# Linear-memory attention and a leaky two-layer network in one Trainium2 kernel: another layout for phi, keys and values, and another order at three places

## The chip, the cores and the metric

The kernel runs on one core of one Trainium2 chip. A core has five engines with an instruction queue each: PE (TensorE, the matrix unit; its weight loads are listed apart as PEld), DVE (VectorE), ACT (ScalarE), POOL (GpSimd) and SP (SyncE, which here only issues loads and stores). PE writes to PSUM, which has eight banks; everything else lies in SBUF. The metric is the time of one execution on the device in microseconds (us). The measurement of the kernel before has a median of 709.62 us over three runs (708.53 to 710.71).

## The reference

All inputs are float32, but the two weight matrices, which are float64. B = 8 batches, H = 8 heads, S = 576 tokens, D = 64, M = 32 memory slots, 512 -> 2048 -> 512 for the network.

```python
a = exp(phi - max(phi, axis=2)); a = a / sum(a, axis=2)      # softmax over the 32 slots, per token
k_m = einsum('bhsm,bhsd->bhmd', a, k)                       # keys folded into 32 slots
v_m = einsum('bhsm,bhsd->bhmd', a, v)                       # values folded into 32 slots
scores = q @ k_m.T / sqrt(64)                               # 576 x 32 per head
attn = softmax(scores)                                      # over the 32 slots
x = (attn @ v_m), heads side by side                        # 4608 tokens x 512
h = x @ w_in;  g = maximum(0.01 * h, h);  out = g @ w_out
```

In the kernel the softmax over phi is taken over tokens (axis 2 of phi is the token axis): a maximum and a sum over the 576 tokens for each of the 256 pairs of head and slot. Values are never multiplied out: `v_m` is folded into `w_in` for each batch, so that the first layer works on `attn` straight away.

## The kernel before

**Steps.** Work is written as small steps with names, and the order in which the program issues them is the order on every engine. The steps of batch b are `a{b}.`:

- `phi`, `kv0`, `kv1`, `q0`, `q1`: the loads, all issued on SP, with 96 partitions of six tokens each (CP = 96, NJ = 6). They go into the pool "ld" of eight buffers, which the pieces of the weights use as well.
- `A1` (DVE): maxima of phi over a partition's six tokens, in five instructions. `A2` (PE): two transposes. `A3` (DVE): the maxima over partitions, put on a diagonal. `B0` (PE): one product that spreads them over all partitions. `B1x` (DVE): subtract. `B2x` (ACT): exponential. `B3` (POOL): sums over the six tokens, in five instructions.
- `C10`, `C11` (PE, L444): the products of exponentials with keys and values, 6 tokens x 4 heads for each of the two head groups g, at four column positions of the array, with 96 rows and 128 columns (keys and values of a head side by side). An fp32 product goes to PE as two pieces, so 48 products stand in the profile as 96. `C2` (PE): two transposes of the sums. `C3` (DVE): reciprocals, the scaled keys `x_k` and the scaled values `x_v`. `C4` (DVE): a bound on the values.
- `D1` (PE): transposes of `x_k` and `x_v`. `D2` to `D6`: scales and copies (`D3` on ACT copies the keys, `D5` the values). `Q0`, `Q1` (DVE): transposes of the queries, written over buffers of the keys and values.
- `E1` (PE, L567): the scores, at 12 positions of the array, three PSUM banks. `E20` to `E22` (DVE): transposes to SBUF. `S{c}{n}`: the second softmax in chunks of 192 columns ("tb"), on DVE for the first chunks of batch 0 and with POOL otherwise.

The weights come in three pieces a matrix: `i0.ld0` is a load of piece 0 of the first quarter of `w_in`, `o0` is for `w_out`; `y` (ACT), `h` (DVE or ACT) and `t` (DVE) turn float64 into float32, `b` (ACT) squares, `k` (ACT) and `l` (DVE) split a weight into two fp16 parts. `f0j.1` and `f0j.2` fold the values of batch 0 into quarter j and keep the result in fp32; `w0.2`, `w1.1`, `w1.2` and the later `fold` do it for the fp16 parts, with `split` on ACT and DVE.

**Groups and units.** The tokens are worked off in 12 groups of 384 (G = 0 to 11), each in eight units u of 256 hidden columns. A unit is: up products (L750, two PSUM buffers "ph"), leaky activation (ACT, then two instructions on DVE for the fp16 parts), down products (L808, three PSUM banks "po"). Group 0 is done in fp32 while the weights still come in, in an order written out by hand (`OPENING`), in which `u0.P0` is the first half of unit 0's up products, `V` the activation and `O` the down products; `z.n` stands for n idle products. From group 1 on everything is fp16 in three products a tile, in slots: `slot(n)` issues the up products of unit n + 3, the fold that is due (`folds`), its activation, and then the down products of unit n. The steps of the next batches are hung into the slots by three tables (`BEFORE`, `AFTER`, `ENDS`), and so are the fp16 splits of the weights (`SPLIT`). A slot in the steady part takes 5.8 us of PE.

**Buffers in PSUM.** The pool "pa" has three banks. `C10` takes two of them (transposed sums, products), `E1` all three, a fold two.

**The end of a group.** `store` copies a bank "po" to SBUF on ACT (two buffers "ob") and issues four stores of 32 rows for it on SP.

Of the kernel before, what the change touches and what calls it, by code (L numbers as in the profile page):

```python
# [22 lines left out]
A_SCALE = 2.0**13  # L23
# [14 lines left out]
z.14 a0.phi a0.kv1 a0.kv0 a0.A1 a0.A2 a0.A3 a0.q0 a0.B0 z.4 a0.B10 a0.q1 a0.B11 a0.B20 a0.B21  # L38
a0.B3 i0.ld0 a0.C10 a0.C11 a0.Q0 a0.C2 z.4 i0.ld1 i0.ld2 a0.C3 o0.ld0 a0.Q1 a0.D1 i0.y0 i0.h0
a0.D3 i0.t0 a0.D5 a0.E1 i0.y1 i0.h1 i0.t1 i0.y2 o0.ld1 o0.ld2 o1.ld0 a0.E20 i0.h2 a0.E21 a0.S01  # L40
o1.ld1 a0.S11 o0.y0 a0.S02 a0.S12 a0.S03 i0.t2 a0.S13 o1.ld2 o0.y1 a0.S04 f00.1 z.6 a0.S14
i1.ld0 f00.2 a0.S05 o0.h0 a0.S15 i1.ld1 a0.S06 o0.h1 a0.S16 u0.Pa0 o0.y2 a0.E22 u0.Pa1 o0.h2
a0.C4 u0.Pb0 o1.y0 o0.t0 u0.Pb1 u0.V0 a0.D2 o0.t1 u0.V1 i1.ld2 u1.Pa0 o1.y1 a0.D4 i2.ld0 u1.Pa1
# [12 lines left out]
o0.k0 u6.O1 o0.k1 o0.k2 w1.2 u7.O1 o0.l0 o0.l1 o0.l2
# [27 lines left out]
IDLE = (4, 6, 14)  # L84


BEFORE = {2: "A3", 3: "B10", 5: "C3 C4", 7: "D4 D3 D5 D6", 8: "E20 E21 E22", 9: "S03", 11: "S07"}
AFTER = {
    0: "A1", 3: "B20 B3", 6: "Q0 Q1", 8: "S01 S02", 9: "S04 S05", 10: "S06", 11: "S08",
}  # L90
ENDS = {1: "A2", 2: "B0", 4: "C10 C11 C2", 6: "D1 D2", 7: "E1"}
# [3 lines left out]
def kernel(  # L95
# [43 lines left out]
    HP = H // NG  # L139
    ND = D // 32  # L140
# [31 lines left out]
    wo = [const.tile([P, WC], F32, name=f"wo{j}") for j in range(NQ + 1)]  # L172
    wi_s, wo_s = (
# [47 lines left out]
    def weights(kind, j, steps, act):  # L221
# [116 lines left out]
    def attention(b, steps, chunks, f32_chunks=0):  # L338
# [632 lines left out]
```

## Time and profile before

| | |
|---|---|
| median of the runs | 709.62 us (708.53 to 710.71) |
| the profiled execution, whole | 707.58 us |
| its span, first to last instruction | 705.8 us |
| mean granted clock of PE | 0.983 |
| PE busy | 680.9 us, 96% |
| DVE, ACT, POOL busy | 391.6, 266.7, 86.3 us |
| read from HBM, written | 49.81 MB, 9.44 MB |

The page of the profile has the busy share of every engine in 40 slices of the span (17.6 us each), as tenths. A timeline line has the start and the length of a run of like instructions, what was read and written, how many there were, and in brackets how long the engine stood idle before and what released it. A window's line has a stretch of time, its length, then for PE, PEld, DVE, ACT and POOL the busy time and the number of instructions, then the granted clock, the share of the 16 DMA engines and GB/s. In the lines of a single line of code stand the least, median and greatest duration in ns and the start of the first and the last. A piece on PE lasts longer than the distance to the next, since pieces run in a pipeline and side by side.

### The profile page before, as it was taken

What the parts mean: (1) busy time and instruction counts of PE and PEld (TensorE: products, weight loads), DVE (VectorE), ACT (ScalarE), POOL (GpSimd) and SP (SyncE); (2) the same over time, 40 slices, a digit from 0 to 9 for tenths busy, and PEclk for the clock granted to TensorE, in tenths of its full rate; (3) what the DMA queues carried; (4) which work ended last, traced back from release to release, by engine and by line L of the source; (5) the groups of instructions that cost most, each with busy time, mean ns of one, the idle gap of its engine ahead of it and who ended that gap; (6) DMA issues with size and microseconds to landing.
All of it is one profiled execution on the core that took longest, in us unless ns stands there. A gap on an engine that the chain in (4) does not pass through costs nothing.

```text
span 705.8 us, 13103 instructions
## 1 busy us (share of the span) xinstructions
PE 680.9 (96%) x5606; PEld 380.0 (54%) x5606; DVE 391.6 (55%) x618; ACT 266.7 (38%) x426; POOL 86.3 (12%) x82
## 2 busy tenths in 40 slices
PE   6799996999999999999999999999999999999995
PEld 5465544665545545565555545665545545665442
DVE  2884586785797573434684664344594664332220
ACT  1499575562562332421331342321242332321211
POOL 2010230020151120020140020010031030000000
PEclk8699999999999999999999999999999999999999
DMA  9999604904513410303513320304410100100101
GB/s 212 362 385 240 227 0 97 217 1 119 140 25 102 123 25 1 79 1 102 143 37 102 99 48 1 79 1 102 106 41 2 42 5 1 46 1 1 46 1 45
DMA packets 38714, 60.10 MB, mean 85 GB/s; under 512 B 4352, under 2 KB 28928, under 8 KB 38656
## 3 DMA queue, kind: packets, MB, share of 16 engines
q1 hardware_dynamic: 38656, 59.26, 31.5%
q8 instruction: 44, 0.72, 0.4%
q14 instruction: 14, 0.11, 0.1%
HBM read 49.81 MB, written 9.44 MB: 84 GB/s over the span
## 4 chain that ended last, share of the span: by engine, by line
PE 86%; DMA 5%; DVE 4%; ACT 3%; SPq 1%; issue 1%; POOL 0%; ACTq 0%; DVEq 0%; POOLq 0%
PE po L808 50%; PE ph L750 25%; PE pa L662 3%; PE pa L444 3%; PE pa L567 2%; DMA ld<-in_v_dram 1%; DMA ld<-in_moe_w_in_dram 1%; DMA out_dram<-ob 1%; ACT ob L779 1%; SPq L786 1%; DMA ld<-in_phi_dram 1%; ACT W L690 1%; DVE W L691 1%; DVE ld L546 0%; PE pa L404 0%
## 5 line engine op out<-in xcount | busy, mean ns | idle before, releaser
L808 PE MATMUL po<-wo,g 128*128 128x512 f16 (+1 forms) x1680 | 400.6, 392 | 0.3
L808 PEld LDWEIGHTS <-g 128*128 128x128 f16 x1584 | 152.5, 98 | 184.3 <-issue 12.7
L750 PE MATMUL ph<-a,W 128*128 128x192 f16 (+3 forms) x1520 | 210.8, 292 | 5.0 <-ACT gf L757 5.0
L757 ACT ACTIVATE gf<-ph,g_sc 128x384 f32<-128x384 f32 x176 | 98.9, 579 | 229.6 <-PE ph L750 164.2
L765 DVE CAST g<-gf 128x768 f16<-128x768 f32 x88 | 59.9, 681 | 192.7 <-ACT gf L757 192.6
L750 PEld LDWEIGHTS <-W 128*128 128x128 f16 x1440 | 130.3, 98 | 59.6 <-issue 4.4
L766 DVE TENSOR_TENSOR g<-gf,g 128x768 f16<-128x768 f32 x88 | 87.4, 993 | 3.1
L600 POOL TENSOR_TENSOR t<-t,tm 128x1152 f32<-128x1152 f32 (+2 forms) x9 | 16.5, 1833 | 232.5 <-DVE tm L597 232.5
L779 ACT ACTIVATE ob<-po,osc 128x512 f32<-128x512 f32 x29 | 19.7, 688 | 58.7 <-DMA out_dram<-ob 31.6
L662 PE MATMUL pa<-wi,vT 64*32 64x512 f16 (+1 forms) x704 | 32.3, 430 | 2.4 <-DVE t L577 1.9
L691 DVE SCALAR_TENSOR_TENSOR W<-pa,W 128x512 f16<-128x512 f32 x48 | 30.8, 683 | 0.0
L546 DVE STREAM_TRANSPOSE ld<-ld 96x1536 f32<-96x1536 f32 x16 | 27.5, 1752 | 5.8 <-DMA ld<-in_q_dram 5.8
L808 PEld LDWEIGHTS po<-wo,g 128*128 128x128 f32 x96 | 17.5, 190 | 20.8 <-issue 18.7
L434 POOL TENSOR_TENSOR r1k<-r1k,ld 96x256 f32<-96x256 f32 x32 | 27.6, 861 | 2.5
L444 PE MATMUL pa<-ld 96*32 96x128 f32 x768 | 24.9, 286 | 2.8 <-DMA ld<-in_v_dram 2.8
L432 POOL TENSOR_TENSOR r1k<-ld 96x256 f32<-96x256 f32 x8 | 6.5, 815 | 171.0 <-ACT ld L422 171.0
L690 ACT ACTIVATE W<-pa 128x512 f16<-128x512 f32 x48 | 26.1, 599 | 2.7 <-PE pa L662 2.6
L257 ACT ACTIVATE ld<-ld 128x768 f32<-128x768 f32 (+1 forms) x24 | 19.9, 844 | 18.9 <-DMA ld<-in_moe_w_in_dram 16.9
L444 PEld LDWEIGHTS pa<-ld 96*32 96x32 f32 x768 | 22.2, 115 | 7.4 <-issue 3.3
L633 POOL TENSOR_TENSOR a<-t,a 128x1152 f16<-128x1152 f32 (+2 forms) x9 | 18.0, 1999 | 41.4 <-ACT a L629 41.4
L605 ACT ACTIVATE t<-t 128x1152 f32<-128x1152 f32 (+2 forms) x11 | 9.9, 904 | 30.7 <-POOL t L600 30.6
L577 DVE STREAM_TRANSPOSE t<-pa 128x384 f32<-128x384 f32 x24 | 12.3, 556 | 14.3 <-PE pa L567 14.3
(138 smaller groups left out, 421.3 us busy)
## 6 DMA issues: line engine op xcount, KB each, us to landing
ld<-in_k_dram SPq DMA_DIRECT2D x32, 288.0 KB, 5.4
ld<-in_v_dram SPq DMA_DIRECT2D x32, 288.0 KB, 5.7
ld<-in_q_dram SPq DMA_DIRECT2D x16, 576.0 KB, 6.7
out_dram<-ob SPq DMA_DIRECT2D x144, 64.0 KB, 1.7
ld<-in_moe_w_in_dram SPq DMA_DIRECT2D x12, 512.0 KB, 6.2
ld<-in_moe_w_out_dram SPq DMA_DIRECT2D x12, 512.0 KB, 7.2
ld<-in_phi_dram SPq DMA_DIRECT2D x8, 576.0 KB, 7.0
ld<-in_moe_w_in_dram SPq DMA_DIRECT2D x8, 256.0 KB, 7.4
```

The costliest lines, as they stand in the source:

```text
L434: nc.gpsimd.tensor_tensor(s0, s0, ph[:, :, :, j, :], ALU.add)
L444: nc.tensor.matmul(pk[hh * M:(hh + 1) * M, g, :, :], ld["phi"][:, 2 * hh + g, j, :], ld["kv", g, hh // 2][:, :, hh % 2, j, :], start=(j == ...
L546: nc.vector.transpose(flat, ld["q", g].rearrange("p hh j d -> p (hh j d)"))
L662: nc.tensor.matmul(pf[g][cols, :], lhs, rhs, start=(n == 0), stop=(n == len(passes) - 1), tile_position=(g * D, hh * M),)
L690: nc.scalar.activation(w[:, g, 0], src[g], AF.Copy, scale=ws)
L691: nc.vector.scalar_tensor_tensor(w[:, g, 1], src[g], ws, w[:, g, 0], ALU.mult, ALU.subtract)
L750: nc.tensor.matmul(ph[:, t0:t0 + n * SB], lhs, rhs, start=(m == 0), stop=(m == len(seq) - 1))
L757: nc.scalar.activation(dst, ph, AF.Prelu, scale=sc, alpha=SLOPE)
L765: nc.vector.tensor_copy(g[:, 0], gf)
L766: nc.vector.tensor_tensor(g[:, 1], gf, g[:, 0], ALU.subtract)
L779: nc.scalar.activation(ob, po, AF.Copy, scale=so)
L808: nc.tensor.matmul(po, lhs, rhs, start=(f == 0 and m == 0), stop=(f == NQ * NF - 1 and m == len(seq) - 1),)
```

## The change

Phi, keys and values are laid out anew: a head's 576 tokens now fill 64 partitions with nine tokens each (KJ = 9), and the two heads of a pair (hh, g) fill the lower and upper 64 partitions, so all 128 are used. With it

- `A1` and `B3` become one reduction on DVE each (batch 0: `A10` and `A11` for two halves of phi, which are loaded one after the other);
- `A2` and `C2` become one transpose; `B0` becomes two products at two column positions;
- `C10` has 9 x 4 x 2 = 72 products with 64 rows, at four column positions in each of two row halves, into one PSUM bank for each g. For batch 0 keys and values are done apart, `C10` for keys and `C11` for values;
- `C3` is `C30` (DVE, reciprocals), `C3k` (`x_k`, now on ACT) and `C31` (`x_v`, two instructions); `D1` is `D10` and `D11`.

Phi, keys and values of batch 0 are loaded into weight tiles that are not yet in use, and in the order phi, keys, queries, the first quarter of `w_in`, values. `OPENING` is written anew (the idle products too: `z.14` first, then 2, 4, 4, 2, 5, 2, 4), batch 0's first fp32 chunk has two "tb" in place of two chunks of one, and a unit's up products are no longer cut in two halves of tokens. The scales of the folded weights are made once (`fold_scales`) and not in each `split`. At the begin of group 1 the slots issue up products of unit n + 2, none in slot 8, two units in slots 9 and 11. `store` has three buffers, and the stores of the last group go out on SP, POOL and ACT, a bank each.

```diff
-BEFORE = {2: "A3", 3: "B10", 5: "C3 C4", 7: "D4 D3 D5 D6", 8: "E20 E21 E22", 9: "S03", 11: "S07"}
+BEFORE = {
+    2: "A3", 3: "B10", 4: "B3", 5: "C30 C3k C31 C4", 7: "D4 D3 D5 D6", 8: "E20 E21 E22",
+    9: "S03", 11: "S07",
+}
...
+        phi_rows = phi[b].rearrange("h s m -> (h s) m").rearrange(
+            "(hh gp j) m -> gp hh j m", gp=P, j=KJ
+        )
...
-            for j in range(2, NJ):
-                nc.vector.tensor_tensor(mx, mx, phi_t[:, :, j, :], ALU.max)
+            nc.vector.tensor_reduce(
+                var["mx"][:, h0:h1], ld["phi"][:, h0:h1].rearrange("p hh j m -> p hh m j"),
+                AX.X, ALU.max,
+            )
...
+            for g in range(NG):
+                nc.tensor.matmul(
+                    pb[g * D:(g + 1) * D].rearrange("p hh m -> p (hh m)"), ones[:, :D],
+                    var["diag"][:, g], start=True, stop=True, tile_position=(0, g * D),
+                )
...
+            for j in range(KJ):
                 for hh in range(HP):
-                        pk[hh * M:(hh + 1) * M, g, :, :],
-                        ld["phi"][:, 2 * hh + g, j, :],
-                        ld["kv", g, hh // 2][:, :, hh % 2, j, :],
-                        start=(j == 0), stop=(j == NJ - 1), tile_position=(0, hh * M),
+                    for g in range(NG):
+                        rows = slice(g * D, (g + 1) * D)
+                        nc.tensor.matmul(
+                            var["pk"][g][hh * M:(hh + 1) * M, cs], ld["phi"][rows, hh, j, :],
+                            ld["kv", hh][rows, kinds[0]:kinds[-1] + 1, j, :],
+                            start=(j == 0), stop=(j == KJ - 1), tile_position=(g * D, hh * M),
+                        )
...
-                nc.vector.tensor_scalar(
+                nc.scalar.activation(
                     x_k[:, g],
...
+                    AF.Copy, scale=var["r2"][:, 1, g:g + 1],
...
-        ob = ffn.tile([P, E], F32, name="ob", bufs=2)
+        ob = ffn.tile([P, E], F32, name="ob", bufs=3)
+        last = G == len(units) // NU - 1
+        eng = (nc.sync, nc.gpsimd, nc.scalar)[t] if last else nc.sync
...
     def slot(n):
-        m = n + UA
+        if n < NU:
+            ms = [n + 2]
+        else:
+            ms = {NU: [], NU + 1: [n + 1, n + 2], NU + 2: [n + 2], NU + 3: [n + 2, n + 3]}.get(
+                n, [n + UA]
+            )
```

More of the change, by code (lines that the diff above doesn't have):

```diff
@@ L37 @@
 OPENING = """
[L38 to L43, printed above, removed]
@@ L56 @@
-o0.k0 u6.O1 o0.k1 o0.k2 w1.2 u7.O1 o0.l0 o0.l1 o0.l2
+z.14 a0.phi0 a0.phi1 a0.k a0.q0 a0.A10 a0.A11 a0.q1 a0.A2 z.2 a0.A3 a0.B0 z.4 i0.ld0 a0.B10
+a0.B11 a0.B20 a0.B21 i0.ld1 a0.C10 a0.B3 a0.Q0 a0.C2 z.4 i0.ld2 a0.v a0.C30 a0.Q1 a0.C3k a0.D10
+z.2 i0.y0 i0.h0 a0.D3 i0.t0 o0.ld0 a0.E1 z.5 i0.h1 i0.y1 i0.t1 o0.ld1 i0.y2 a0.E20 i0.h2 a0.E21
+i0.t2 o0.ld2 a0.S01 i0.b o1.ld0 a0.E22 a0.C11 z.2 a0.S02 a0.C31 a0.S03 o1.ld1 a0.S11 a0.D11
+o0.y0 a0.S04 a0.S12 a0.D5 o0.h0 o1.ld2 f00.1 z.4 a0.S05 a0.S13 i1.ld0 f00.2 a0.S06 o0.y1 a0.C4
@@ L422, in exp_phi @@
+        def exp_phi(js):
+            part = ld["phi"][:, :, js, :]
             nc.scalar.activation(part, part, AF.Exp)
-        for i in range(parts):
-            steps[f"{name}B1{i}"] = lambda i=i: sub_max(i)
-            steps[f"{name}B2{i}"] = lambda i=i: exp_phi(i)
+        for i in range(len(half) - 1):
+            js = slice(half[i], half[i + 1])
+            steps[f"{name}B1{i}"] = lambda js=js: sub_max(js)
+            steps[f"{name}B2{i}"] = lambda js=js: exp_phi(js)
         @step("B3")
@@ L478, in _ @@
                 )
+        @step("C31")
+        def _():
             var["x_v"] = x_v = att.tile([P, NG, D], F32, name="x_v", bufs=2)
-            nc.vector.tensor_tensor(
-                x_v, pk[:, :, 1, :], r2.unsqueeze(2).broadcast_to([P, NG, D]), ALU.mult
-            )
+            for g in range(NG):
+                nc.vector.tensor_scalar_mul(
+                    x_v[:, g], var["pk"][g][:, D:2 * D], var["r2"][:, 0, g:g + 1]
+                )
         @step("C4")
@@ L722, with up_products @@
     gs = {}
[L724 to L727 removed]
+    def up_products(G, u, i):
+        ph = ps_h.tile([P, GT], F32, name="ph")
         (b0, tb0), (b1, tb1) = blocks(G)
[L729 to L731 removed]
+        if b0 == b1:
             parts = [(b0, tb0, 2, 0)]
@@ L894 @@
         if b + 1 < B:
-            put(ends, n0 + 5, b + 1, "phi kv0 kv1")
+            put(ends, n0 + 5, b + 1, "phi kv0 kv1 kv2 kv3")
             put(ends, n0 + 8, b + 1, "q0 q1")
@@ L917, in slot @@
     def slot(n):
-        m = n + UA
-        rest = []
-        if m < len(units):
+        if n < NU:
+            ms = [n + 2]
+        else:
+            ms = {NU: [], NU + 1: [n + 1, n + 2], NU + 2: [n + 2], NU + 3: [n + 2, n + 3]}.get(
+                n, [n + UA]
+            )
+        rest = []
+        if not ms or ms[0] >= len(units):
+            run(before.get(n, ()))
+        for m in ms:
+            if not NU <= m < len(units):
+                continue
             phs = [up_products(*units[m], i) for i in range(2)]
-            rest = [(b, j, fold(b, j)) for b, j in folds(m)]
-        run(before.get(n, ()))
-        if m < len(units):
+            rest += [(b, j, fold(b, j)) for b, j in folds(m)]
+            if m == ms[0]:
+                run(before.get(n, ()))
             activate(*units[m], phs)
@@ L937 @@
         run(OPENING.split())
-        run(["a2.phi", "a2.kv0", "a2.kv1", "a2.q0", "a2.q1"])
+        run([f"a2.{key}" for key in "phi kv0 kv1 kv2 kv3 q0 q1".split()])
         for n in range(NU - UA, len(units)):
```

223 lines of the change are left out of this document (115 added, 108 removed).

## The prediction

> **What bounds the kernel now.** I read the page first, then the timeline of TensorE over the opening and over the begin of the second group, then the chain of waits and the windows of 5 us there, then single lines in the steady part, and last the end.
>
> ```profile
> span 705.8 us, 13103 instructions
> ...
> PE 680.9 (96%) x5606; PEld 380.0 (54%) x5606; DVE 391.6 (55%) x618; ACT 266.7 (38%) x426; POOL 86.3 (12%) x82
> ...
> PE   6799996999999999999999999999999999999995
> ...
> PEclk8699999999999999999999999999999999999999
> ```
>
> TensorE is busy for 680.9 of 705.8 us. A change can win only in three ways: less work for PE, an earlier start of the dense part (slices 1 and 2 show 6 and 7, and a clock of 0.6 in the second), or removal of the dip in the seventh slice (6). The other engines have room over the whole span. PE's timeline of the opening:
>
> ```profile
> 0.99 5.97 PE L864 MATMUL pa<-ones 128*128 128x128 f32 x28 [0.99 <-POOL ones L165]
> 8.54 0.36 PE L389 MATMUL pa<-ident,r1k 96*128 96x96 f32 x2 [1.58 <-DVE r1k L382]
> 9.96 1.17 PE L404 MATMUL pa<-r1k,ones 128*96 128x256 f32 x2 [1.06 <-DVE r1k L399]
> ...
> 13.62 0.41 PE L444 MATMUL pa<-ld 96*32 96x128 f32 x4 [0.79 <-DMA ld<-in_v_dram]
> 16.02 4.48 PE L444 MATMUL pa<-ld 96*32 96x128 f32 x92 [1.98 <-DMA ld<-in_v_dram]
> ...
> 22.21 0.66 PE L499 MATMUL pa<-ident,x_k 128*96 128x128 f32 x4 [0.48 <-DVE x_k L473]
> ...
> 24.46 1.96 PE L567 MATMUL pa<-ld,kT 32*32 32x192 f32 x96 [1.43 <-ACT kT L513]
> ...
> 31.22 1.92 PE L662 MATMUL pa<-wi,vT 64*32 64x512 f32 x4 [0.49 <-DVE wi L266]
> 33.81 2.93 PE L864 MATMUL pa<-ones 128*128 128x128 f32 x12 [0.67 <-ACT W L678]
> 36.53 3.07 PE L750 MATMUL ph<-a,W 128*128 128x192 f32 x16
> ```
>
> Until 36.53 us, where the first up products start, PE mostly waits: for phi and its maxima (8.54), for the softmax of phi (13.62), for the last of keys and values (16.02), for the scores' operands (24.46), and for the first weight matrix (31.22). From 36.53 on it has work in hand until 106 us. The chain of waits and three windows say what delays the weights:
>
> ```profile
> 20.52 0.16 SPq L236
> ...
> 20.73 5.02 DMA ld<-in_moe_w_in_dram
> ```
>
> ```profile
> 10.00:15.00 5.00, 3.25 (x14) 2.48 (x14) 1.81 (x2) 1.69 (x2) 1.77 (x3) 0.67 1.10 245
> ...
> 35.00:40.00 5.00, 5.00 (x30) 5.00 (x29) 2.75 (x7) 3.63 (x7) 0.00 (x0) 0.79 1.03 401
> ...
> 45.00:50.00 5.00, 5.00 (x13) 1.93 (x11) 4.79 (x8) 5.00 (x7) 0.00 (x0) 1.00 0.95 347
> ```
>
> The second piece of the first weight matrix is issued only at 20.5 us, when the products of keys and values release a buffer of the pool "ld". While keys, values and queries travel (10 to 15 us; 96 partitions), the 16 engines are full (1.10) at 245 GB/s. While weights travel (128 partitions), they move 401.
>
> **The opening.** I follow the new order with the old durations.
>
> ```profile
> 6.16 0.42 DVE L380 TENSOR_TENSOR r1k<-ld 96x256 f32<-96x256 f32 x1 [6.16 <-DMA ld<-in_phi_dram]
> ```
>
> The 28 pieces of idle products still end at 6.96 us; phi in two halves, reduced by two instructions, should be ready by then (old phi started its five maxima at 6.16, and they ended at 8.4). So A2 goes at 7.0 instead of 8.54. A2 to B0 takes 1.42 as before: 8.4. B0 to the end of the exponentials took 3.66 with 1536 columns, and it is 1152 now, 0.75 of it: C10 at 11.2. It needs keys alone, and phi and keys (1.77 MB) at 245 GB/s need 7.2 us, so they have landed even with 3 us of latency. C10 is now 72 products as 144 pieces (below) in some 2.6 us, but B3 and the first flip of queries stand on DVE in that time, so C30 starts at 14.3 and x_k, now on ACT, is done at 16.4. D10 to E1 took 2.25: E1 at 18.6, against 24.46. From E1 to the first up products it was 12.07, the last 2.72 of it idle products behind the late weights. That piece lies between 9.4 (without them) and 14.1 (with 2.6 for the products of the values, which now stand between); weights no longer wait for a buffer, since phi, keys and values of batch 0 live in weight tiles. I take 11.0: first up products at 29.6, a gain of **6.9 us**, with 2.5 to 9 as its bounds.
>
> Behind that point PE has the same work; ACT, 5.00 of 5.00 busy at 45 to 50 us, has the same conversions of weights to make and starts them only as early as the loads land, so I take off 1.0 for new waits there. Batch 1 saves as each later batch does (0.7). Opening: **6.6**.
>
> **The second group.**
>
> ```profile
> 113.40 2.14 PE L750 MATMUL ph<-a,W 128*128 128x192 f16 x24
> 115.47 1.09 PE L662 MATMUL pa<-wi,vT 64*32 64x512 f32 x16
> 116.92 2.14 PE L750 MATMUL ph<-a,W 128*128 128x192 f16 x24 [0.35 <-ACT gf L757]
> 123.26 3.40 PE L750 MATMUL ph<-a,W 128*128 128x192 f16 x24 [4.20 <-ACT gf L757]
> ...
> 129.60 4.05 PE L808 MATMUL po<-wo,g 128*128 128x512 f16 x18
> 134.09 2.14 PE L750 MATMUL ph<-a,W 128*128 128x192 f16 x24 [0.43 <-ACT gf L757]
> ```
>
> ```profile
> 119.09 1.33 ACT L690 ACTIVATE W<-W,ws 128x512 f16<-128x512 f32 x2 [1.75 <-DVE ws L685]
> 121.47 1.26 ACT L690 ACTIVATE W<-pa,ws 128x512 f16<-128x512 f32 x2 [1.05 <-DVE ws L685]
> ```
>
> From 113.40 to 134.09 PE does four blocks of up products (2.0 each, start to start), two folds (1.0 each) and one block of down products (3.9): 13.9 of 20.7 us. 6.8 are lost, above all the 4.2 before 123.26, where ACT first splits two folded weights (each waits for a scale from DVE) and then frees the buffer; after it the clock had fallen and 24 products took 3.40 instead of 2.14. The new slots put the block of down products of unit 0 in front of the third block of up products, the scales are made once, and the third store waits for no DMA. What is late next: the splits of the following folds, behind the activations of two units in one slot. ACT needs 1.3 for each of two splits and DVE follows, some 4 us after the last activation; PE has 3.9 of down products to cover that. I leave 1.8 lost: gain **5.0**, bounds 2 (the 4.2 come back) and 6.8.
>
> **Batches 2 to 7.** The rows of a single execution of C10 and C11 together, of E1, and of one fold, and two steps of the chain:
>
> ```profile
> L444 PE MATMUL pa<-ld x96: 272/273/297, 159.4 to 161.9; 96*32 96x128 f32 x96
> ```
>
> ```profile
> L567 PE MATMUL pa<-ld,kT x96: 321/321/345, 180.7 to 182.3; 32*32 32x192 f32 x96
> ```
>
> ```profile
> L662 PE MATMUL pa<-wi,vT x24: 376/376/387, 202.9 to 203.3; 64*32 64x512 f16 x24
> ```
>
> ```profile
> 65.48 0.17 PE pa L389 x2
> ...
> 68.25 0.43 PE pa L404 x2
> ```
>
> Now 48 products go as 96 pieces, four side by side: 24 rounds in some 2.5 + 0.27 us, 0.11 a round, 26 ns a piece. Then 72 products go as 144 pieces, eight side by side: 18 rounds. The trace has no such run of fp32 products over both row halves. From below: 18 rounds at 0.11 are 2.0 us. From above: 144 at 26 ns are 3.8. E1, twelve side by side, goes at (182.3 - 180.7) / 95 = 17 ns a piece (at C10's pace its 192 columns would need 0.165 a round, 14 ns); the fold, with the very same half rows, has 24 in 0.4 us. E1 is nearest in kind (many small fp32 pieces): 144 x 17 = 2.4, a gain of 0.35.
>
> The Trainium skill, page "TensorE: Matmul & The Clock Gate", section "Wait — 56ns, not 53.3ns?", says that start to start never drops below about 25 ns however small a product is; by it C10 would take 3.6 us, an estimate, and each batch would lose 0.85 there. By that rule E1 could not have gone at 17 ns, so the trace does not agree for tiles side by side.
>
> B0 (0.43) halves, as its two halves of columns stand side by side: 0.21. A2 and C2 have one transpose for two (0.17 now): 0.07 each. Together **0.7 a batch, 4.2 for six**, bounds -4 (3.8 us for C10) and 6.6.
>
> What moves off PE's path:
>
> ```profile
> L597 DVE TENSOR_REDUCE tm<-t 128x36 f32<-128x1152 f32 x6 | 8.1, 1346 | 0.0
> ...
> L382 DVE TENSOR_TENSOR r1k<-r1k,ld 96x256 f32<-96x256 f32 x32 | 18.9, 591 | 1.1
> ...
> L473 DVE TENSOR_SCALAR x_k<-pa,r 128x192 f32<-128x192 f32 x16 | 5.9, 413 | 0.3
> ```
>
> A1 goes from five instructions (0.45 + 4 x 0.59 is 2.8 us) to one reduction of 1152 columns (1.35); B3 costs DVE 1.35 that POOL had; x_k takes 0.8 from DVE and gives it to ACT; C30 and C31 have two small instructions more (0.3). DVE saves about 0.6 a batch, ACT gains about 0.5. Both lie under PE's 5.8 us a slot. The one new wait: C30 and x_k now stand in front of a slot's activations on ACT, and with a fold in the same slot (batches 3, 5, 7) PE's second fold bank is the bank of the keys' products, free only after C30 (1.0), x_k's first half (0.4) and x_v's. That is 1.5 us behind C2, and the up products in between take 2.0. If DVE is late by more than that 0.5, PE waits; I book nothing and keep 1.5 us for the range. Loads keep their eight issues a batch on SP.
>
> **The end.**
>
> ```profile
> 697.41 1.33 ACT L779 ACTIVATE ob<-po,osc 128x512 f32<-128x512 f32 x2 [13.66 <-PE po L808]
> 698.12 5.56 SPq L786 DMA_DIRECT2D out_dram<-ob  x12
> 701.25 0.69 ACT L779 ACTIVATE ob<-po,osc 128x512 f32<-128x512 f32 x1 [2.50 <-DMA out_dram<-ob]
> ```
>
> The third eviction waits 2.50 for a buffer. With three buffers it ends at 699.4 instead of 701.9, and its four stores, issued on ACT, need not queue behind eight others. The stores on POOL have no row here: if an issue costs there what it costs on SP (5.56 / 12 is 0.46), they are issued by 700.6; at three times that by 704.3, and nothing is won. I take **2.2**, bounds 0 and 2.6.
>
> **Sum.** 6.6 + 5.0 + 4.2 + 2.2 = 18.0. The profiled execution took 707.58 us (span 705.8 and 1.8 around it), 2.04 below the median of 709.62; 689.6 against the one is **691.6** against the other, which I forecast.
>
> **The rivals.**
> *ACT holds the opening.* PE starts at 29.6, but conversions of weights keep it waiting: for it speaks ACT's 5.00 of 5.00, against it that loads come sooner and that ACT is idle before 20 us. Opening gain 2.5: 695.7. Chance 0.15.
> *The second group's wait moves.* The splits of the next folds stop PE for the old 4 us two slots later: gain 2, 694.6. For it: DVE and ACT make the same splits. Chance 0.10.
> *The pace of pieces stays 26 ns.* C10 takes 3.8 instead of 2.4, seven times: 691.6 + 9.8 = 701.4. Against it: E1's 17 ns and the fold. Chance 0.08. The rule of the Trainium skill's page "TensorE: Matmul & The Clock Gate" (3.6 us) gives nearly the same, 700.0, and its chance lies within this one's.
> *The loads gain nothing.* 128 partitions move at 245 GB/s like 96: values land some 3 us later, and the first up products wait as long: 694.6. Chance 0.05.
> *Slower than before.* Each change between row halves, which the new loop makes at every product, lets the array run empty. If each piece then takes what a round takes now, 0.11, 144 are 15.7 us, 13 more a batch, 7 times: 691.6 + 93 = 785. It turns slower from 35 ns a piece (18.0 - 2.4 = 15.6 saved elsewhere, by 7 and by 144, above 2.75 / 144 = 19). Against it: the fold alternates the same halves and starts 24 pieces in 0.4 us. Chance 0.03.
>
> **How the numbers follow.** The forecast has 0.59. A measurement of this kernel tells 0.3% (2.1 us) from no change. All cases but the last are faster; I put 0.94 on faster, 0.02 on the same (several bounds falling together), 0.04 on slower. The range goes down to 684 (opening 9, second group 6.8, 6.6 for the batches, 2.6 at the end is 25 less) and up to 700, which holds the first two rivals and the fourth and leaves most of the third out.
>
> **What would show it.** E1 near 18.6 us and the first up products near 29.6; the second and third piece of the first weights issued before 12 us; no wait over 2 us for PE between 100 and 135 us and a full clock there; 144 pieces of C10 in some 2.4 us, at 17 ns; slots of 5.8 us elsewhere unchanged; the third eviction right behind the second and a tail of 6 us instead of 8.4. I am wrong if PE shows a wait above 3 us in the opening's dense part, or C10 above 2.8 us.

## The result and the profile after

The changed kernel takes 688.43 us (median; 687.76 to 691.03) beside 710.0 (708.53 to 710.71) of the kernel before: a ratio of 0.9706, 95% interval 0.9675 to 0.9737, 21.6 us by the medians. 691.6 was forecast, and 684 to 700 as range. The profiled execution took 691.03 us, the longest of the four, where that of before lay 2 us below its median; the two spans therefore show only 16.6 of the 21.6 us.

The page of the changed kernel:

```profile
span 689.2 us, 14081 instructions
...
PE 672.7 (98%) x6136; PEld 371.0 (54%) x6136; DVE 390.7 (57%) x582; ACT 269.3 (39%) x441; POOL 54.9 (8%) x46
...
PE   6799999999999999999999999999999999999996
...
PEclk9699999999999999999999999999999999999999
...
q8 instruction: 48, 0.79, 0.5%
```

The dip in the seventh slice is gone. The second slice still shows a clock of 0.6, and the queue row at the end (packets, MB, share) will matter for the opening. TensorE's timeline of the opening, and three windows (length, busy time of PE, PEld, DVE, ACT, POOL, then clock, DMA share, GB/s):

```profile
18.82 1.78 PE L613 MATMUL pa<-wi,kT 32*32 32x192 f32 x46 [1.96 <-ACT kT L560]
...
20.12 1.95 PE L613 MATMUL pa<-wo,kT 32*32 32x192 f32 x46
22.56 2.51 PE L908 MATMUL pa<-ones 128*128 128x128 f32 x10 [0.49 <-DVE t L623]
...
28.83 1.09 PE L710 MATMUL pa<-wi,vT 64*32 64x512 f32 x16 [0.35 <-ACT vT L566]
31.24 1.79 PE L908 MATMUL pa<-ones 128*128 128x128 f32 x8 [1.32 <-issue]
32.82 2.54 PE L794 MATMUL ph<-a,W 128*128 128x384 f32 x4
```

```profile
15.00:20.00 5.00, 2.36 (x49) 1.83 (x61) 3.87 (x5) 2.78 (x5) 0.00 (x0) 0.79 1.04 399
20.00:25.00 5.00, 4.51 (x79) 3.47 (x55) 4.03 (x7) 2.93 (x4) 0.00 (x0) 0.50 1.04 398
25.00:30.00 5.00, 4.57 (x166) 3.25 (x165) 3.34 (x8) 3.70 (x7) 0.87 (x2) 0.68 1.04 403
```

E1 starts at 18.82, where 18.6 was forecast, but at half clock it lasts until 22.07 (3.3 us, where it took 1.96 before), PE then waits 0.49 us, and the first up products start at 32.82 instead of 36.53. The begin of the second group:

```profile
109.38 2.14 PE L794 MATMUL ph<-a,W 128*128 128x192 f16 x24
111.45 1.09 PE L710 MATMUL pa<-wi,vT 64*32 64x512 f32 x16
112.47 2.15 PE L794 MATMUL ph<-a,W 128*128 128x192 f16 x24
114.46 4.05 PE L854 MATMUL po<-wo,g 128*128 128x512 f16 x18
118.35 2.14 PE L794 MATMUL ph<-a,W 128*128 128x192 f16 x24
120.42 1.09 PE L710 MATMUL pa<-wi,vT 64*32 64x512 f32 x16
121.44 2.15 PE L794 MATMUL ph<-a,W 128*128 128x192 f16 x24
123.43 4.05 PE L854 MATMUL po<-wo,g 128*128 128x512 f16 x18
127.32 0.27 PE L420 MATMUL pa<-ident,r1k 128*128 128x128 f32 x1
127.43 2.40 PE L794 MATMUL ph<-a,W 128*128 128x192 f16 x24
```

No row but the last shows a loss; seven steps take 123.43 - 109.38 = 14.1 us, 20.7 before. From the first up products of this group to C10 of batch 2 it is 39.6 us (109.4 to 149.0), 46.0 before (113.4 to 159.4). C10 itself in one execution (ns shortest/median/longest, first and last start), then the groups that cost VectorE more or less than was thought:

```profile
L478 PE MATMUL pa<-ld x144: 268/269/294, 149.0 to 150.9; 64*32 64x128 f32 x144
```

```profile
L478 PE MATMUL pa<-ld 64*32 64x128 f32 x1008 | 16.0, 271 | 1.1 <-issue 1.1
L406 DVE TENSOR_REDUCE r1k<-ld 128x128 f32<-128x1152 f32 x7 | 15.1, 2158 | 0.0
L461 DVE TENSOR_REDUCE r1k<-ld 128x128 f32<-128x1152 f32 x7 | 15.1, 2156 | 1.2 <-ACT ld L451 1.2
...
L643 DVE TENSOR_REDUCE tm<-t 128x36 f32<-128x1152 f32 x6 | 8.1, 1346 | 0.0
```

From its first start to the next instruction's, C10 takes 2.18 us (2.76 before): 15.1 ns a piece. The end:

```profile
681.95 1.98 ACT L823 ACTIVATE ob<-po,osc 128x512 f32<-128x512 f32 x3 [13.66 <-PE po L854]
682.66 1.72 SPq L832 DMA_DIRECT2D out_dram<-ob  x4
683.60 2.13 POOL L832 DMA_DIRECT2D out_dram<-ob  x4 [115.74 <-ACT ob L823]
683.96 1.88 ACTq L832 DMA_DIRECT2D out_dram<-ob  x4
```

The three evictions stand back to back, and all stores are issued by 685.8; the span ends 3.4 us later.

The four stretches between the same places of both traces: to the begin of the second group 113.4 to 109.4 (4.0 less), from there to C10 of batch 2 46.0 to 39.6 (6.4 less), from there to the last block of down products 523.6 to 518.5 (5.1 less), and the rest 22.8 to 21.7 (1.1 less).

### The profile page after: what moved, and what is told of

It is laid out like the page before. It is cut to its first block, busy times and chain, and to the rows that moved or that the text cites. A ratio compares the mean times of both kernels' runs of the same rounds, so it can differ in the third digit from the quotient of the medians.

```text
span 689.2 us, 14081 instructions
## 1 busy us (share of the span) xinstructions
PE 672.7 (98%) x6136; PEld 371.0 (54%) x6136; DVE 390.7 (57%) x582; ACT 269.3 (39%) x441; POOL 54.9 (8%) x46
## 4 chain that ended last, share of the span: by engine, by line
PE 95%; DMA 2%; SPq 1%; DVE 1%; issue 1%; ACT 0%; POOL 0%; POOLq 0%; ACTq 0%
PE po L854 55%; PE ph L794 28%; PE pa L710 4%; PE pa L613 2%; PE pa L478 2%; DMA ld<-in_moe_w_in_dram 2%; PE pa L908 1%; PE pa L543 0%; DVE W L734 0%; PE pa L436 0%; PE po L478 0%; PE pa L211 0%; SPq L379 0%; PE pa L492 0%; POOL out_dram L832 0%
## 5 line engine op out<-in xcount | busy, mean ns | idle before, releaser
L794 PE MATMUL ph<-a,W 128*128 128x192 f16 (+2 forms) x1504 | 211.1, 294 | 0.1
L809 DVE CAST g<-gf 128x768 f16<-128x768 f32 x88 | 61.7, 701 | 190.5 <-ACT gf L801 190.4
L810 DVE TENSOR_TENSOR g<-gf,g 128x768 f16<-128x768 f32 x88 | 84.3, 958 | 3.1
L646 POOL TENSOR_TENSOR t<-t,tm 128x1152 f32<-128x1152 f32 (+2 forms) x9 | 15.9, 1768 | 438.7 <-DVE tm L643 438.7
L854 PEld LDWEIGHTS po<-wo,g 128*128 128x128 f32 x96 | 17.9, 190 | 21.5 <-issue 20.2
L710 PE MATMUL pa<-wi,vT 64*32 64x512 f16 (+1 forms) x704 | 28.9, 420 | 0.4 <-ACT vT L566 0.4
L593 DVE STREAM_TRANSPOSE ld<-ld 96x1536 f32<-96x1536 f32 x14 | 24.1, 1752 | 0.2 <-DMA ld<-in_q_dram 0.2
L513 ACT ACTIVATE x_k<-pa,r 128x192 f32<-128x192 f32 x14 | 5.1, 416 | 38.2 <-PE ph L794 38.2
L677 ACT CAST a<-t 128x1152 f16<-128x1152 f32 (+2 forms) x9 | 8.8, 974 | 26.2 <-DVE t L673 26.2
L478 PE MATMUL pa<-ld 64*32 64x128 f32 x1008 | 16.0, 271 | 1.1 <-issue 1.1
L908 PE MATMUL pa<-ones 128*128 128x128 f32 x74 | 13.8, 351 | 2.8 <-issue 1.3
```

What stands on the lines that cost most here:

```text
L478: nc.tensor.matmul(var["pk"][g][hh * M:(hh + 1) * M, cs], ld["phi"][rows, hh, j, :], ld["kv", hh][rows, kinds[0]:kinds[-1] + 1, j, :], sta ...
L593: nc.vector.transpose(flat, ld["q", g].rearrange("p hh j d -> p (hh j d)"))
L710: nc.tensor.matmul(pf[g][cols, :], lhs, rhs, start=(n == 0), stop=(n == len(passes) - 1), tile_position=(g * D, hh * M),)
L794: nc.tensor.matmul(ph[:, t0:t0 + n * SB], lhs, rhs, start=(m == 0), stop=(m == len(seq) - 1))
L809: nc.vector.tensor_copy(g[:, 0], gf)
L810: nc.vector.tensor_tensor(g[:, 1], gf, g[:, 0], ALU.subtract)
```

## The experiments

All are edits of the changed kernel. Medians in us; the ratio is against the kernel before, run in the same series.

| kernel | time | before | ratio (95%) |
|---|---|---|---|
| e1 old begin | 690.07 | 711.1 | 0.9714 (0.9687 to 0.9741) |
| e2 halves apart | 697.55 | 711.1 | 0.9817 (0.9792 to 0.9842) |
| e3 POOL first | 689.21 | 711.1 | 0.9701 (0.9678 to 0.9725) |
| e4 stores on SP, two buffers | 695.26 | 711.1 | 0.9785 (0.9759 to 0.9811) |
| e5 old begin, two buffers | 696.09 | 710.83 | 0.9800 (0.9776 to 0.9824) |
| e6 the same, scales in the folds | 700.81 | 710.83 | 0.9869 (0.9847 to 0.9891) |
| e7 more idle products | 692.23 | 710.83 | 0.9747 (0.9731 to 0.9764) |
| e8 opening reordered | 689.14 | 710.83 | 0.9706 (0.9688 to 0.9724) |
| e9 wide idle products | 686.99 | 710.39 | 0.9673 (0.9653 to 0.9692) |
| e10 reordered, wide, filled | 688.39 | 710.39 | 0.9686 (0.9663 to 0.9709) |
| e11 scales in the folds only | 693.33 | 710.39 | 0.9769 (0.9742 to 0.9796) |
| e12 the changed kernel again | 689.55 | 710.39 | 0.9699 (0.9675 to 0.9723) |

e12 is the measure for the others:

> The changed kernel once more, unchanged, as the measure for the other kernels of this call: 687.5 to 690 us; first up products at 32 to 33 us, the second group from 107.3 to 109.4, the clock at half from 17 to 26 us, the two pauses in front of PE's instructions 961 and 1473.

It behaved so: first up products at 32.9, second group from 107.9, span 687.8.

### What removed the second group's wait

The theory of the forecast put the new order first, the scales and the third buffer beside it. e1 puts back the order alone.

```diff
-            ms = {NU: [], NU + 1: [n + 1, n + 2], NU + 2: [n + 2], NU + 3: [n + 2, n + 3]}.get(
-                n, [n + UA]
-            )
+            ms = [n + UA]
```

> Only the order of the second group's first slots is put back: each slot again issues the up products three units ahead, and the down products of unit (1,0) come behind the third block of up products. Opening, attention loop and end stay as in the changed kernel. Theory (the order itself removed the wait): from the first up products of the second group to the seventh step PE takes 20.7 us again instead of 14.1, with a wait near 4 us before the third block, and the time rises by 5 to 6.6 us over the changed kernel. Rival (the scales made once, and not the order, removed the wait): less than 2 us. Rival (the wait had moved to later slots, which now get it back): less than 3 us in all, with a window of 5 us behind the seventh step that shows less idle PE than in the changed kernel.

The theory fell. TensorE's timeline of e1:

```profile
107.24 2.14 PE L794 MATMUL ph<-a,W 128*128 128x192 f16 x24
...
113.82 2.14 PE L794 MATMUL ph<-a,W 128*128 128x192 f16 x24 [1.33 <-ACT gf L801]
...
122.79 2.14 PE L794 MATMUL ph<-a,W 128*128 128x192 f16 x24
```

One wait of 1.33 us is left, and seven steps take 15.5 us. The order is worth 1.2 to 1.5 us, not 5. e5 adds two buffers in place of three (`bufs=2` for `ob`), e6 adds the scales made in each `split`:

```diff
-    ws = states[b]["ws"][:, j:j + 1] if b < FB else W_FOLD
+    ws = W_FOLD
+    if b < FB:
+        ws = sm.tile([P, 1], F32, name="ws")
+        nc.vector.tensor_scalar(
+            ws, states[b]["rv"], sw[:, j:j + 1], A_SCALE / W_SPLIT, ALU.mult, ALU.mult
+        )
```

> The old order of the second group's first slots and two output buffers instead of three; the last stores stay on three queues. With the old order alone the seven steps took 15.5 us, with two buffers and the new order 14.4, in the changed kernel 14.1, in the kernel before 20.7. Theory (the third eviction of the first group, which waits 2.5 us for a store, holds ScalarE and so the first activations, and the old order has nothing to cover that): the seven steps take 18.5 to 20.7 us, with a wait of 3 us or more for PE. Rival (the two are independent): 15.9 us. Rival (the scales made at each fold set the wait): 16 to 17 us here, and the rest only in the kernel that also makes the scales at each fold.

> As the kernel with the old order and two buffers, and the scale of each fold is made on VectorE in front of that fold's split again, instead of once for all four. Theory (ScalarE is held by the store): at most 0.7 us over the kernel without this edit, 0.21 for each of three small instructions. Rival (the scales set the wait): 3 to 5 us over it, and 20.7 us for the seven steps only here.

e5 takes 16.3 us for the seven steps, close to the sum of the two single effects (15.9), and not 18.5 or more. e6 brings the whole wait back, 21.0 us and 4.7 us more time than e5: my theory of both kernels fell, and the scales set the wait. TensorE and ScalarE of e6:

```profile
112.29 2.14 PE L795 MATMUL ph<-a,W 128*128 128x192 f16 x24 [0.30 <-ACT gf L802]
118.64 3.79 PE L795 MATMUL ph<-a,W 128*128 128x192 f16 x24 [4.20 <-ACT gf L802]
```

```profile
114.46 1.33 ACT L738 ACTIVATE W<-W,ws 128x512 f16<-128x512 f32 x2 [1.75 <-DVE ws L733]
116.85 1.27 ACT L738 ACTIVATE W<-pa,ws 128x512 f16<-128x512 f32 x2 [1.05 <-DVE ws L733]
118.00 1.06 ACT L802 ACTIVATE gf<-ph,g_sc 128x384 f32<-128x384 f32 x2
```

This is the trace of before again, to the 4.20. The scale itself takes 0.21 us on VectorE, but stands there behind the residual of the activations, and the second scale behind the residual of the first split. So ScalarE waits 1.75 + 1.05 us for VectorE, and the activations that free PE's banks stand behind it. e11 makes the scales in the folds and leaves the new order and three buffers:

> The changed kernel with one thing undone: the scale of each fold of the second group is made on VectorE in front of that fold's split, not once for all four. With the old order and two buffers this cost 4.7 us. Theory (ScalarE and VectorE wait for each other in turn: the second split of a pair may start only when VectorE has finished the first, 2.4 us later; the block of down products that the new order puts between covers only part of it): the seven steps take 15 to 17 us instead of 14.1. Rival (the new order covers it wholly): 14.1 to 14.6. Rival (it costs the same everywhere): 18.5 to 19.

Its seven steps take 14.7 us, which is what I would have called success; the wait has moved to the eighth:

```profile
127.45 0.26 PE L795 MATMUL ph<-a,W 128*128 128x192 f16 x1 [0.27 <-ACT W L738]
128.24 0.42 PE L795 MATMUL ph<-a,W 128*128 128x192 f16 x3 [0.53 <-DVE W L739]
128.90 0.34 PE L795 MATMUL ph<-a,W 128*128 128x192 f16 x2 [0.24 <-DVE W L739]
129.74 0.26 PE L795 MATMUL ph<-a,W 128*128 128x192 f16 x1 [0.51 <-ACT W L738]
130.53 0.42 PE L795 MATMUL ph<-a,W 128*128 128x192 f16 x3 [0.53 <-DVE W L739]
```

These 24 products take 5.0 us start to start instead of 2.0: the forecast's rival "the second group's wait moves", two slots later as it said. Over the whole stretch from the first up products to C10 of batch 2:

| edit undone | stretch, us | over the changed kernel |
|---|---|---|
| none (three executions) | 39.6 | |
| buffers (e4) | 40.3 | 0.7 |
| order (e1) | 40.8 | 1.2 |
| order and buffers (e5) | 41.6 | 2.0 |
| scales (e11) | 43.4 | 3.8 |
| all three (e6) | 46.3 | 6.7 |

The single effects add up to 5.7 of 6.7, and e6 is within 0.3 of the kernel before (46.0). e11's time is 3.8 us over e12's: nothing is given back later.

### What the row halves are worth

e2 goes through one half after the other:

```diff
-            for j in range(KJ):
-                for hh in range(HP):
-                    for g in range(NG):
+            for g in range(NG):
+                for j in range(KJ):
+                    for hh in range(HP):
```

> The loop over the two row halves is put outside in the products of keys and values, so that four tiles stand side by side instead of eight; same products, same pieces, same data. Theory (a round of tiles side by side costs the same 0.11 us, whether four or eight stand in it): 36 rounds instead of 18, 3.9 us per batch instead of 2.18, 1.7 more for each of seven batches, so 10 to 12 us over the changed kernel. Rival (the pieces are started one by one at 15 us per thousand, and how many stand side by side does not matter): 2.2 us per batch still, within 1 us of the changed kernel. Rival (a floor of 25 ns between starts): 3.6 us in both, which the changed kernel's own 2.18 already speaks against.

The group of C10's pieces in e2:

```profile
L478 PE MATMUL pa<-ld 64*32 64x128 f32 x1008 | 26.2, 271 | 0.0
```

The same 1008 pieces of the same 271 ns cost 26.2 us of PE instead of 16.0. One C10 takes 3.68 us, 36 rounds of 0.102; with eight side by side it is 18 rounds of 0.121. So the theory holds (3.9 was expected), a fuller round being a fifth dearer; but at least some 25 ns from start to start within one row half would give e2 the same time, and no run tells the two apart. The kernel is 8.3 us slower than e3, its neighbour in the series, where 10 to 12 was expected: 1.5 in each of six batches, but only 0.4 in batch 1, whose C10 had a pause in e3 (see the opening). The order of the loop carries the gain: with the halves apart C10 would be 0.9 us slower than the one it replaced.

### The end

```diff
-        eng = (nc.sync, nc.gpsimd, nc.scalar)[t] if last else nc.sync
+        eng = (nc.gpsimd, nc.sync, nc.scalar)[t] if last else nc.sync
```

> Only the queues of the last twelve stores are exchanged: GpSimd's queue gets the first output bank instead of the second, SyncE's the second. Theory (GpSimd's stores and what GpSimd does behind them end last): they are issued from 682.9 instead of 683.6 in the changed kernel's times, all is over 0.6 us sooner, and the stretch from the last up products to the end of the span falls from 21.7 to 21.1 us. Rival (ScalarE's stores, which land 2.8 us after their issue, end at the same time anyway): within 0.2 us of 21.7.

From the last block of down products to the end of the span it is 21.5 us, 21.7 in the changed kernel: the rival holds within its 0.2. In the changed kernel the last stores on GpSimd's and ScalarE's queues land 2.7 and 2.8 us after their issue (median), those on SyncE's, which go first, 1.7. In e3, where the three queues store side by side, SyncE's take 2.3 and the others 2.8 and 2.7, so the lateness is not that of two queues alone, and it is of no use to exchange them.

e4 has `bufs=2` and `eng = nc.sync` for all:

> The end is put back as it was: two output buffers, and all twelve last stores on SyncE's queue. Theory: the third eviction waits some 2.5 us for a buffer, and the stretch from the last up products to the end of the span is 22.8 us again instead of 21.7: 1.1 us over the changed kernel. Rival (the 2.2 us of the forecast, hidden in the profiled execution by its own scatter): 2.2 us.

Both were wrong by far: 6.0 us over e3. The end accounts for 1.5 of them (23.0 us). Of the rest, 0.7 is in the begin of the second group (table above), 1.0 in this execution's opening, and 3.1 in six blocks of down products that wait at the begin of later groups. The view of waits counts the three longest (us in all, times, longest); below it is the last of them:

```profile
PE po L854 <- ACT ob L823: 1.9, 3, 1.4
```

```profile
647.53 0.69 ACT L823 ACTIVATE ob<-po,osc 128x512 f32<-128x512 f32 x1 [3.86 <-DMA out_dram<-ob]
...
648.27 2.75 PE L854 MATMUL po<-wo,g 128*128 128x512 f16 x12 [1.44 <-ACT ob L823]
```

The third eviction of every group waits for a store to free its buffer, and the next group's down products wait for the bank. The third buffer removes that; I had looked for its worth at the end alone. The kernel before lost less here (four blocks 0.2 us late, 0.9 in all); why the same wait is longer in e4 is open.

### The opening

Three things were left to explain: the half clock, the 1.32 us of "issue" before 31.24, and one like it in batch 1's C10 (TensorE of the changed kernel):

```profile
65.69 2.01 PE L478 MATMUL pa<-ld 64*32 64x128 f32 x127
68.82 0.48 PE L478 MATMUL pa<-ld 64*32 64x128 f32 x17 [1.12 <-issue]
```

e7 fills the two gaps ahead of E1:

```diff
-a0.C10 a0.B3 a0.Q0 a0.C2 z.4 i0.ld2 a0.v a0.C30 a0.Q1 a0.C3k a0.D10
-z.2 i0.y0 i0.h0 a0.D3 i0.t0
+a0.C10 a0.B3 a0.Q0 a0.C2 z.12 i0.ld2 a0.v a0.C30 a0.Q1 a0.C3k a0.D10
+z.10 i0.y0 i0.h0 a0.D3 i0.t0
```

> More idle products in the opening: 24 pieces instead of 8 behind the row sums of batch 0, and 20 instead of 4 in front of its scores; they end before the scores' operands are there, so the order of the work is the same. Theory (the clock falls to half from 17 to 26 us because PE stands idle from 13.8 to 18.8): the scores of batch 0 run at a full clock in 1.9 us instead of 3.7, and the first up products start 1.5 to 2 us before 32.1. Rival (the clock falls at that time whatever PE does, or falls because it does more): scores in 3.7 us still, first up products within 0.4 us of 32.1.

The clock is 1.00 in every window from 10 to 30 us, and E1 takes 1.9 us instead of 3.3 (the 3.7 of the expectation counts to the next instruction; it is 2.5 here): the theory holds for the clock. Still the kernel is some 3 us slower, because of something else. Its chain of waits:

```profile
24.13 1.47 PE po L478 x87
25.60 4.73 issue
30.33 0.33 PE po L478 x11
```

PE stands still for 4.7 us in the middle of the products of the values, waiting for nothing the profile shows. In all traces with the changed kernel's PE instructions a long pause stands at the 961st of them, and in all but e2 at the 1473rd, if PE's waits for semaphores are counted too (of weight loads and products alone they are the 955th and the 1456th); e7 has 64 more idle instructions, and the pause is again at the 961st, which is now another piece of work. e8 leaves the clock alone and shortens the chain to the first up products (the sequence of DVE's and ACT's steps between E1 and u0.P0, and no `z.5`, no `z.4`):

```diff
-z.2 i0.y0 i0.h0 a0.D3 i0.t0 o0.ld0 a0.E1 z.5 i0.h1 i0.y1 i0.t1 o0.ld1 i0.y2 a0.E20 i0.h2 a0.E21
...
+z.2 a0.D3 i0.y0 i0.h0 i0.t0 o0.ld0 a0.E1 i0.h1 i0.y1 i0.t1 o0.ld1 i0.y2 a0.E20 i0.h2 a0.E21
+a0.S01 i0.t2 o0.ld2 i0.b o1.ld0 a0.C11 z.2 a0.S02 a0.E22 a0.S03 a0.C31 o1.ld1 a0.D11
+a0.D5 o0.y0 a0.S04 f00.1 o1.ld2 a0.S05 i1.ld0 f00.2 a0.S06 a0.S11 a0.S12 o0.h0 a0.S13 o0.y1 a0.C4
```

> Only the order of the opening between the scores and the first up products of batch 0 is changed: the copy of the transposed keys stands ahead of the first conversion of weights on ScalarE, the products of the values follow the scores without idle products between, the third flip and the values' scaling stand behind steps of the softmax on VectorE, and the idle products ahead of the first up products are left out. Theory (the first up products wait for this chain, in which the copy waits 1.8 us behind a conversion, the softmax 1.3 us for the products of the values, and the up products 0.7 us for idle products): first up products at 29.5 to 30.5 us instead of 32.1, and 1.5 to 2.5 us less in all. Rival (the conversions of weights set the pace of the opening): first up products earlier, but the second group still begins within 0.5 us of 107.3. Rival (the clock stays at half for longer without idle products): less than 1 us won at the first up products.

First up products at 30.2, as the theory has it, and second group at 107.1, as the first rival has it; yet the reason is the clock, as in the second rival, whose number (less than 1 us won) fails: the first 16 up products take 7.5 us instead of 5.4 in e3 (clock 0.66 from 30 to 35 us), and the first down products start at 37.7, 37.5 in e3. The 1.9 us won are lost to the clock.

e9 keeps the changed kernel's order and makes the idle products four times as wide and a quarter as many, a hundred PE instructions fewer:

```diff
-        for _ in range(n):
-            nc.tensor.matmul(pi, ones, ones, start=True, stop=True)
+        for x in range(0, n, 4):
+            m = min(4, n - x)
+            nc.tensor.matmul(
+                pi[:, 0:m], ones, ones.unsqueeze(1).broadcast_to([P, m, P]), start=True, stop=True
+            )
```

> Every idle product of the opening takes up to four times the columns, and there are a quarter as many: the same columns, a hundred TensorE instructions fewer ahead of the first up products; the order stays that of the changed kernel. In every trace so far PE stands still in front of its instructions 961 and 1473 (weight loads and products counted together), 512 apart: 1.9 to 2.3 us ahead of the idle products in front of the first up products, 1.1 to 1.4 us inside batch 1's products of keys and values. Theory (the pause belongs to the number of the instruction, so that it must move to others): no pause above 0.3 us inside batch 1's products, 2.2 us for them instead of 3.3; the idle products in front of the first up products start 0.5 to 1 us sooner, and the first up products at 31.2 to 31.8 instead of 32.1; 1 to 1.5 us less in all. Rival (the pause belongs to the work: a bank or an operand that is late): both pauses stay where they are, within 0.4 us.

Both pauses are gone: C10 of batch 1 takes 2.18 us, and behind 27.41 there is no "issue". TensorE of e9, and two of its windows:

```profile
27.41 1.12 PE L909 MATMUL pa<-ones 128*128 128x512 f32 x2
29.67 1.53 PE L794 MATMUL ph<-a,W 128*128 128x384 f32 x4 [1.13 <-DVE a L668]
```

```profile
15.00:20.00 5.00, 3.10 (x102) 2.07 (x102) 4.39 (x8) 3.13 (x6) 0.00 (x0) 1.00 1.04 398
20.00:25.00 5.00, 3.19 (x148) 2.26 (x148) 4.30 (x7) 3.79 (x5) 0.00 (x0) 1.00 1.05 401
```

A pause of 0.7 us stands at PE's 705th instruction instead, 256 before the 961st, among the products of the values. The pause belongs to the instruction's number, not to the work. First up products at 29.67, second group from 103.8, 686.99 us: 2.6 us below e12 by the medians (its five runs 686.19 to 687.62, e12's 687.34 to 690.14), more than the 1 to 1.5 expected. The profiled execution, the fastest, also kept its clock (a mean of 0.999); the other four have 0.991 to 0.995 and e12's five 0.989 to 0.991, so the clock explains a part of it, and how large a part is open. Two small pauses remain inside C10 of batches 6 and 7 (0.3 and 0.6 us longer). This is the fastest kernel of the study.

e10 joins the wide products to a new order that fills every gap, and e3's stores. In short:

```diff
+z.3 a0.D3 i0.y0 i0.h0 i0.t0 o0.ld0 a0.E1 i0.h1 i0.y1 o0.ld1 a0.E20 z.8 a0.E21 a0.S01 i0.t1
+i0.y2 i0.h2 o0.ld2 o1.ld0 a0.C11 z.4 a0.S02 a0.E22 i0.t2 a0.S03 a0.C31 o1.ld1 a0.D11 a0.D5 a0.S04
+o0.y0 f00.1 z.5 o1.ld2 a0.S05 i1.ld0 f00.2 a0.S06 a0.S11 a0.S12 i0.b o0.h0 a0.S13 o0.y1 a0.C4
```

> The mended order of the opening, wide idle products that fill PE's pauses from 13 us on, the flips of the scores ahead of the second conversion of weights, and the first output bank on GpSimd's queue. Theory (the clock falls because PE stands idle, and the mended chain is shorter): clock above 0.95 from 10 to 35 us, scores of batch 0 in 2 us, first up products at 28 to 29.5 us at 325 ns each, second group from 104 to 105.5 instead of 107.3, and 2 to 3.5 us less than the changed kernel. Rival (the conversions of weights set the pace once PE starts sooner): first up products as early, but the second group from 106.5 or later, less than 1 us in all. Rival (the clock falls whatever PE does): a clock of 0.7 or less in one window of 5 us before 35 us.

The clock is 1.00 in every window and the first up products start at 29.4. Then ScalarE is late: it has the squares (`i0.b`, 1.9 us) and conversions in front of the first activation.

```profile
34.72 1.56 PE L794 MATMUL ph<-a,W 128*128 128x384 f32 x4 [1.72 <-ACT g L801]
```

The second group begins at 106.6, as the first rival said. It gains 1.2 us over e12 by the medians, within their scatter.

## Why the prediction was right, and where it was not

**The opening, 6.6 forecast.** 4.0 in the profiled execution, 5.5 in e12, 6.1 in e3; the term holds in size, with its largest part missed and made up for behind. The first up products came 3.7 us sooner (4.4 in e3) and not 6.9; from them to the second group it is 76.6 us (75.2 in e3), 76.9 before, so that the 1.0 taken off for new waits there was not lost. E1 came at 18.8 (18.6), but by errors that cancel. C10 starts at 9.5 and not at 11.2, and lasts 2.1 us and not 2.6. Behind it VectorE is busy with B3 (2.2 us) and the flip of the queries until 14.3, where the forecast has C30 too. From D10 to E1 it is then 3.1 us and not 2.25, because the copy of the keys stands on ScalarE behind the conversion of the first weights, which land at 17.3. "E1 to the first up products 11.0" failed: 14.0 (its upper bound of 14.1 is mis-added, 12.07 and 2.6 are 14.7). That step took E1 at full speed (1.9), and counted waits on loads alone. The runs show in its place E1 at half clock (3.3, with 2.5 for the ten idle pieces behind it) and the pause at the 961st instruction. With both gone, e9 has its first up products at 29.67, where 29.6 was forecast; that agreement is luck, since E1 starts at 17.65 there and the piece takes 12.0 us, not 11.0. Behind E1, conversions of weights did not hold PE in the changed kernel (that rival is seen only in e10).

**The second group, 5.0 forecast.** 6.4; the bound was 6.8. The mechanism quoted from the trace, splits that wait for a scale from DVE, was right. The step that named the block of down products as the cover, and left 1.8 us lost for the next splits, had the weights wrong: the scales bring 3.8, the order 1.2, the buffer 0.7. Without the wait for scales the splits leave 0.35 us (the row at 127.43).

**Batches 2 to 7, 4.2 forecast.** The stretch behind C10 of batch 2 shows 5.1 less, of which 0.9 are waits for output buffers that I had not seen. In C10, 17 ns a piece was nearest by kind but not exact: 15.1, or 13.8 counted from first to last start as the 17 was; 0.58 saved and not 0.35. The Trainium skill, page "TensorE: Matmul & The Clock Gate", section "Wait — 56ns, not 53.3ns?", gives about 25 ns as the least from start to start; here eight tiles side by side went at 15.1, and only e2's four at 25.5 (3.68 us by 144). B0 was mis-sized the other way: its two halves stand side by side, but the four pieces take 0.37 us, not 0.21. A2 and C2 gave 0.06 each, as forecast. Not on PE's path, but wrong: A1 and B3 were priced at 1.35 from a reduction of as many elements; over the strided view they take 2.16, so DVE, which was to save 0.6 a batch, is as busy as before (390.7 us, 391.6 before). Behind 140 us this cost nothing: the view of waits lists none for PE there.

**The end, 2.2 forecast.** 1.1. The third eviction does stand right behind the second. What failed is the silent step that stores on three queues land as soon as those on SP alone; the last of them take 2.8 us and not 1.7, and from the first eviction to the end it is 7.3 us (8.4 before; 6 forecast).

**The sum** (18.0 against 21.6 by the medians, 16.6 and 18.0 by the spans of the changed kernel and of e12) is right within what single executions differ, but that is in part luck: the missed gains, 1.4 in the second group and some 0.9 in the steady part, stood against the missed losses, 0.5 (e3) to 2.6 in the opening and 1.1 at the end. The rivals "pace of 26 ns", "array runs empty" and "loads gain nothing" fell: C10 at 15.1 ns, and values there when C11 starts (e8 and e9 reach C11 sooner and wait for them there; they land at 22.84 in e9). The sign "C10 above 2.8 us" showed once, in batch 1 (3.6 us), by the pause at the 1473rd instruction and not by the pace.

## What to carry to other kernels

A small operation that two engines hand to and fro costs what stands in front of it on each engine, not its own time: 0.21 us of scales cost 3.8 us, and a reorder that seems to remove the wait may only move it two slots on, so measure over a stretch that is longer than the wait's next place. When several edits go into one place, undo each alone before one of them is given the credit. Where PE pauses for "issue", count its instructions, its waits for semaphores among them: if other work stands at the same number in another kernel, make the instructions fewer.

## What was not expected of the hardware

**PE pauses for its code.** Nine traces have the changed kernel's PE instructions at the begin. In all of them PE stops at its 961st instruction (1.3 to 2.5 us from start to start), and in all but e2 at the 1473rd, 512 later (0.7 to 1.7). The row "q8 instruction" shows that code comes by DMA: 48 packets and 0.79 MB for 12,272 weight loads and products are 64 bytes for one, and some 256 in a packet. The times of these packets in the traces show what PE waits for. In the changed kernel the third packet travels from 28.83 to 29.92 us, and PE goes on at 31.24; the fifth from 66.20 to 67.42, and PE goes on at 68.82. The fourteen traces have 654 places like these, at the 449th instruction and each 256 further (waits for semaphores counted). At none of them does PE go on less than 1.2 us after its packet has ended. At 23 the distance from start to start is above 0.55 us, and each of these pauses ends 1.2 to 1.6 us after the packet; at the other 631 it is 0.52 at most. That PE waits for code is thereby shown.

Why the packet is late is not shown. In the nine traces the third one starts 2.7 to 3.7 us after PE has passed the 705th instruction, while loads fill the DMA engines (1.03 to 1.05 from 20 to 30 us). The fifth, where there is a pause, starts 0.6 to 1.5 us after PE has passed the 1217th, with a DMA share of 0.09 to 0.39 from 65 to 70 us; there the pace is enough, since C10 uses up 256 instructions in 2 us. That the loads make the difference is argued: no run changed them. In e2 the fifth packet starts 0.8 us before PE is at the 1217th, and the pause is not there; why is open. The Trainium skill, page "Runtime: NRT & Kernel Launch", section "Instruction fetch mechanics", has code streamed in blocks of 256 instructions, the cost of a boundary "mostly hidden"; the traces agree on the packets, and show the boundaries that are not hidden.

**The clock's fall goes with a late E1.** With the changed kernel's idle products, E1 that started at 17.8 and 18.1 us (e5, e11) left a clock of 0.83 and 0.85 in the window from 20 to 25 us; E1 that started from 18.7 on (seven traces) 0.50 to 0.54, although PE was then busy for 4.1 to 4.5 of the 5 us. That the late start makes the clock fall is not shown: in e1, e2, e3 and e12 the window from 15 to 20 us already has 0.56 to 0.68, so that the fall came before E1. What decides is open. E1's start scatters by 2 us with the same order, because the copy of the keys stands on ScalarE behind the conversion of the first weights, which waits for their load (the changed kernel's chain: weights until 17.3, conversion 0.92, copy, E1).
